# First MLP block by plain products while the weights come; loads, roundings and the first attention in an order written out by hand

## The chip, the cores and the metric

The kernel runs on one core of a Trainium2 chip. Time is device microseconds of one execution. Three timed runs of the kernel before stand beside one execution recorded by the hardware profiler, whose timeline is called the trace. The core's engines work from queues of their own and wait for each other by semaphores: TensorE (PE, with its weight loads PEld), VectorE (DVE), ScalarE (ACT), GpSimd (POOL) and SyncE (SP), which here only issues DMAs.

## The reference

A linear attention without softmax is followed by a two-layer MLP with a leaky ReLU. Batch 8, 8 heads, 576 tokens, head size 64; the MLP sees 4608 tokens of 512 features, 2048 hidden.

```python
kv  = np.einsum('bhsd,bhse->bhde', k, v)
out = np.einsum('bhsd,bhde->bhse', q, kv)
rms = np.sqrt(np.mean(out * out, axis=-1, keepdims=True) + 1e-06)
x   = (out / rms * g_norm).astype(np.float32)       # then (B,H,S,D) -> (B*S, H*D)
h = x @ w_in
g = np.maximum(0.01 * h, h)
return (g @ w_out).astype(np.float32)
```

q, k, v and the result are float32. The weights w_in and w_out come as float64, 8 MB each, and have to be turned into float32 on the chip.

## The kernel before

**Tokens and blocks.** The 4608 tokens are worked off in nine blocks of 512 (`NT`), the eight batches of attention have 576 tokens each, so batch b ends in block b+1. x of a block is kept transposed, `xT` (features on partitions, four sub-tiles `e`, 512 tokens as columns).

**Attention (`attention(b)`, a generator).** Heads go in four pairs p. `load_pair(b, p)` (L87) issues, on SP, two DMAs for k, two for v, and four for q; q is fetched twice, once shifted by 32 columns, so that the DVE's transpose of 32x32 blocks (L198) yields `qT`. Per pair ten small matmuls add up `kv_ps`; a copy (L213) puts it into a block-diagonal `kv`. For each of two pieces of the batch (its columns in block b and in block b+1) four groups of matmuls give `o_ps`; ACT squares it (`sq`, L227) and scales it into `xT` (L228), DVE adds the squares up (L232), a matmul with a matrix of ones (`ss_ps`) sums them per head, ACT takes the root (`rms`, L238), DVE the reciprocal (L239) and the product (L240).

**Weights (`weights()`, a generator).** There are 32 jobs. A job is 512 KB of float64 (`raw`, pool `stage`, two buffers, loaded by SP, L133) that becomes a quarter of one of the 128x1024 tiles `w1`/`w2`. `round_f64` (L120) does this with integer arithmetic: two ACT operations (`add`, `cut`, L137 and L139) and four DVE operations (L140 to L145). Chunk c of the hidden features needs eight jobs in this order: `w1` of half 0 (two jobs), `w1` of half 1 (two), `w2` of half 0 (two), `w2` of half 1 (two).

**MLP.** Each block is computed by a form of Strassen's scheme: `product_h(c)` makes seven products of four 128x256 matmuls from sums of the four quarters of w_in (`sides_w1` on POOL) and of x (`sides_x` on DVE, L245), `product_o(c)` likewise seven from sums of g and w_out. A block has four chunks c, so 56 products. PSUM banks `ha hb hc oa ob oc` hold the products, two more are the attention's.

**What sets the order.** Generators are advanced by `go(steps, n)`. The main loop interleaves `product_h(c)` of a block with `product_o` of the chunk before, one or two steps of the next batch's attention, and, in block 0, the weights. Only the matmuls are held in program order (`keep_in_program_order`); everything else is put in order by the framework's scheduler, which goes by its own estimates. Each engine then executes its list strictly in that order, and a DMA on SP waits there until its target buffer is free. At the start, four rounds of one weight job and two attention steps are written, then the rest of the attention, then the loop.

Of the kernel before, what the change touches and what calls it, by code (L numbers as in the profile page):

```python
# [7 lines left out]
F32 = mybir.dt.float32  # L8
# [12 lines left out]
def kernel(  # L21
# [49 lines left out]
    stage = ctx.enter_context(tc.tile_pool(name="stage", bufs=2))  # L71
# [8 lines left out]

    def matmul(*args, **kw):
        tc.keep_in_program_order(nc.tensor.matmul(*args, **kw))  # L82


    k_ins, v_ins, q_ins = {}, {}, {}

    def load_pair(b, p):  # L87

        for name, src, to in (("k", k, k_ins), ("v", v, v_ins)):
            t = ins.tile([P, 2, JJ, D], F32, tag=f"{name}_in", name=f"{name}_in")
            hs = slice(2 * p, 2 * p + 2)
            nc.sync.dma_start(
                t[:64], src[b, hs, :SLO, :].rearrange("h (p j) d -> p h j d", j=JJ))
            nc.sync.dma_start(
                t[64:, :, :J], src[b, hs, SLO:, :].rearrange("h (p j) d -> p h j d", j=J))
            to[b, p] = t
        t = ins.tile([P, T * D], F32, tag="q_in", name="q_in")
        for l in range(2):  # L100
            for c in range(2):
                r0, n = 64 * l + 32 * c, T * D - 32 * c
                src = q[b, 2 * p + l].rearrange("(t s) d -> t (s d)", s=T)
                nc.sync.dma_start(t[r0:r0 + 32, :n], src[:, 32 * c:])
        q_ins[b, p] = t
# [15 lines left out]
    def round_f64(dst, src):  # L121

        a, n = dst.shape[1:]
        raw = stage.tile([P, a, n, 2], U32, tag="raw", name="raw")
        nc.sync.dma_start(raw.rearrange("p a n two -> p a (n two)"), src.bitcast(U32))  # L133
        raw = raw.rearrange("p a n two -> p (a n) two")
        lo, hi = raw[:, :, 0], raw[:, :, 1]
        add = work.tile([P, a * n], U32, tag="t2k", name="add", bufs=5)
        nc.scalar.activation(add, lo, func=AF.Copy, scale=2.0 ** -29)  # L137
        cut = work.tile([P, a * n], F32, tag="t2k", name="cut", bufs=5)
        nc.scalar.activation(cut, hi.bitcast(F32), func=AF.Copy, scale=2.0 ** -112)  # L139
        nc.vector.tensor_scalar(cut, cut, HIGH_MOST, -HIGH_MOST, op0=ALU.min, op1=ALU.max)  # L140
        tmp = work.tile([P, a * n], U32, tag="t2k", name="tmp", bufs=5)
        nc.vector.tensor_scalar(tmp, cut.bitcast(U32), 3, None, op0=ALU.logical_shift_left)  # L142
        nc.vector.scalar_tensor_tensor(tmp, in0=cut.bitcast(U32), scalar=0x80000000, in1=tmp,  # L143
                                       op0=ALU.bitwise_and, op1=ALU.bitwise_or)
        nc.vector.tensor_tensor(dst.bitcast(U32), tmp.rearrange("p (a n) -> p a n", a=a),  # L145
                                add.rearrange("p (a n) -> p a n", a=a), op=ALU.add)

    w_in_e = w_in.rearrange("(p e) f -> p e f", e=NE)
    w_out_u = w_out.rearrange("(h c u p) m -> h c p u m", h=2, c=NC, p=P)

    def weights():

        for c in range(NC):
            jobs = []
            for h in range(2):
                f0 = h * (DF // 2) + c * U * P
                jobs += [(w1_sb[h][c][:, 2 * a:2 * a + 2, :],
                          w_in_e[:, 2 * a:2 * a + 2, f0:f0 + U * P]) for a in range(2)]
            for h in range(2):
                jobs += [(w2_sb[h][c][:, u:u + 1, :], w_out_u[h, c, :, u:u + 1, :])  # L160
                         for u in range(U)]
            for dst, src in jobs:
                if w_in.dtype == I64:
                    round_f64(dst, src)
                else:
                    nc.sync.dma_start(dst, src)
                yield

    eps_sb = consts.tile([P, 1], F32, name="eps_sb")
    nc.vector.memset(eps_sb, EPS)  # L170

# [19 lines left out]

    def attention(b):

        qT = work.tile([P, NP, S], F32, tag="qT", name="qT")
        kv_ps = ps_att.tile([P, NP, D], F32, tag="att", name="kv_ps")
        for p in range(NP):
            k_in, v_in, q_in = (x.pop((b, p)) for x in (k_ins, v_ins, q_ins))
# [3 lines left out]
            for j in range(JJ):  # L201
                n = P if j < J else 64
                for l in range(2):
                    matmul(kv_ps[64 * l:64 * l + 64, p, :], lhsT=k_in[:n, l, j, :],
                           rhs=v_in[:n, l, j, :], start=(j == 0), stop=(j == JJ - 1))
# [4 lines left out]
        kv = kvs[b % 2]  # L210
        for l in range(2):
            r = slice(64 * l, 64 * l + 64)
            nc.vector.tensor_copy(kv[r, :, :, l, :],  # L213
                                  kv_ps[r].rearrange("p a (i e) -> p a e i", e=NE))
        yield
        for i in (b, b + 1):
            lo, hi = max(i * NT, b * S), min((i + 1) * NT, (b + 1) * S)
            n = hi - lo
            x = block(i)[:, :, lo - i * NT:hi - i * NT]
            sums = None  # L220
            for e in range(NE):
                o_ps = ps_att.tile([P, n], F32, tag="att", name="o_ps")
                for p in range(NP):
# [233 lines left out]
```

## Time and profile before

| | |
|---|---|
| median of three runs (lowest, highest) | 1093.86 us (1093.34, 1098.46) |
| the profiled execution, its own time | 1093.87 us |
| its span, first to last instruction | 1092.2 us |
| mean granted TensorE clock | 0.964 |
| busy: PE, PEld, DVE, ACT, POOL | 992.1, 808.7, 454.0, 270.9, 568.9 us |
| read from HBM, written | 54.27 MB, 9.44 MB |

A line of the timeline reads: start in us from the span's first instruction, duration, engine, line of the code, operation, what is written <- what is read, shape, how many; in brackets the idle time of the engine just before and what ended it. Four fp32 matmuls of 128x256 show as x8, since each is two instructions. A line of the groups ends with busy time in us, mean duration of one in ns, and the idle time of the engine before, with its releasers. A queue (SPq) line is the issuing of DMAs, not their transfer. The rows of stages give length, busy time of PE, PEld, DVE, ACT and POOL with the number of instructions, the granted clock (1.00 is full), the share of DMA busy time and GB/s.

### The profile page before, as it was taken

Reading aid. Unit: us, or ns where it says so; the run is one execution under the profiler, and the core shown is the slowest. Engines: PE = TensorE matmul, PEld = TensorE weight load, DVE = VectorE, ACT = ScalarE, POOL = GpSimd, SP = SyncE. Lnnn points to the kernel's source line nnn. Section 1 sums busy time; section 2 is a strip of 40 time slices with the busy share of each in tenths; the row PEclk is TensorE's granted clock in tenths of the full one; section 3 lists DMA queues with packets and bytes.
Section 4 is the critical chain, followed back from the end, with each engine's and each line's share of the span. In section 5 each row is a group of like instructions: output and inputs, shape, how many; then the busy total and the mean of one; then the engine's idle time right before and its main releaser. Section 6 shows DMA issues by size and latency. Waiting matters only on the chain.

```text
span 1092.2 us, 13409 instructions
## 1 busy us (share of the span) xinstructions
PE 992.1 (91%) x5216; PEld 808.7 (74%) x5216; DVE 454.0 (42%) x617; ACT 270.9 (25%) x498; POOL 568.9 (52%) x441
## 2 busy tenths in 40 slices
PE   2465657999999999999999999999999999999997
PEld 1053445787778877888788878877888788888886
DVE  2485798622462236323632363235322542232223
ACT  0433462113221322122212221222122312111210
POOL 0223334655565556555655565556555655666651
PEclk9686888999999999999999999999999999999999
DMA  8557441240023102310231023101100000001001
GB/s 217 156 142 205 134 153 40 65 118 30 1 65 106 42 1 65 96 52 1 65 96 51 1 65 97 51 1 43 54 30 1 1 10 29 1 1 40 1 1 39
DMA packets 41343, 64.58 MB, mean 59 GB/s; under 512 B 5440, under 2 KB 31040, under 8 KB 41280
## 3 DMA queue, kind: packets, MB, share of 16 engines
q1 hardware_dynamic: 31232, 54.28, 18.2%
q10 hardware_dynamic: 10048, 9.44, 2.6%
q8 instruction: 42, 0.69, 0.3%
q14 instruction: 21, 0.17, 0.1%
HBM read 54.27 MB, written 9.44 MB: 58 GB/s over the span
## 4 chain that ended last, share of the span: by engine, by line
PE 80%; DVE 10%; DMA 4%; issue 2%; ACT 1%; SPq 1%; ACTq 0%; POOL 0%; DVEq 0%
PE h_a L82 22%; PE o_a L82 21%; PE h_c L82 11%; PE o_c L82 10%; PE h_b L82 6%; PE o_b L82 6%; PE o_ps L82 3%; DMA k_in<-in_k_dram 2%; PE kv_ps L82 2%; DVE rms L239 2%; DMA raw<-in_moe_w_in_dram 2%; DVE tmp L143 2%; DVE tmp L142 1%; DVE qT L198 1%; DVE o L245 1%
## 5 line engine op out<-in xcount | busy, mean ns | idle before, releaser
L245 POOL TENSOR_TENSOR wt<-w,wt 128x512 f32<-128x512 f32 x72 | 91.7, 1274 | 151.8 <-PE o_a L82 141.5
L82 PE MATMUL o_a<-wt,gs 128*128 128x256 f32 x576 | 142.5, 391 | 6.7 <-DVE o L245 6.7
L82 PE MATMUL h_a<-xt,ws 128*128 128x256 f32 x576 | 141.9, 390 | 0.0
L245 DVE TENSOR_TENSOR o<-o_a,o 128x512 f32<-128x512 f32 x117 | 80.4, 687 | 143.4 <-PE o_a L82 143.2
L82 PEld LDWEIGHTS o_a<-wt,gs 128*128 128x128 f32 x576 | 106.5, 192 | 37.7 <-issue 19.0
L82 PEld LDWEIGHTS h_a<-xt,ws 128*128 128x128 f32 x576 | 106.9, 192 | 28.0 <-POOL ws L245 7.3
L245 POOL TENSOR_TENSOR gs<-g,g 128x512 f32<-128x512 f32 x72 | 96.6, 1342 | 51.2 <-ACT g L321 47.9
L321 ACT ACTIVATE g<-g 128x512 f32<-128x512 f32 x108 | 68.0, 629 | 147.7 <-DVE g L245 147.5
L245 POOL TENSOR_TENSOR wt<-w,w 128x512 f32<-128x512 f32 x36 | 46.2, 1283 | 98.1 <-PE o_a L82 98.1
L245 POOL TENSOR_TENSOR ws<-ws,w 128x512 f32<-128x512 f32 x36 | 49.6, 1379 | 85.5 <-PE h_a L82 85.2
L245 DVE TENSOR_TENSOR o<-o_c,o 128x512 f32<-128x512 f32 x63 | 43.5, 691 | 95.4 <-PE o_c L82 89.1
L82 PE MATMUL h_a<-xt,w 128*128 128x256 f32 x288 | 70.8, 390 | 9.2 <-DVE g L245 9.2
L82 PE MATMUL h_a<-xT,w 128*128 128x256 f32 x288 | 71.6, 393 | 7.0 <-DVE w L145 7.0
L245 POOL TENSOR_TENSOR ws<-w,w 128x512 f32<-128x512 f32 x36 | 48.3, 1341 | 56.3 <-DVE w L145 55.6
L326 ACT COPY g<-h_a 128x512 f32<-128x512 f32 x36 | 21.1, 585 | 221.7 <-PE h_a L82 209.7
L82 PE MATMUL h_c<-xt,ws 128*128 128x256 f32 x288 | 69.9, 387 | 6.2 <-POOL ws L245 6.2
L245 DVE TENSOR_TENSOR g<-h_b,g 128x512 f32<-128x512 f32 x36 | 24.9, 692 | 115.4 <-PE h_b L82 115.3
L82 PE MATMUL o_a<-wt,g 128*128 128x256 f32 x288 | 68.3, 380 | 2.9 <-DVE o L245 2.9
L82 PE MATMUL o_ps<-qT,kv 128*32 128x64 f32 (+7 forms) x512 | 49.9, 458 | 22.4 <-ACT xT L228 20.8
L82 PEld LDWEIGHTS h_a<-xt,w 128*128 128x128 f32 x288 | 54.8, 194 | 20.3 <-DVE g L245 13.0
L82 PE MATMUL o_c<-wt,gs 128*128 128x256 f32 x288 | 69.1, 383 | 0.0
L82 PE MATMUL o_a<-w,g 128*128 128x256 f32 x288 | 68.1, 379 | 0.8 <-DVE o L245 0.8
(58 smaller groups left out, 1615.2 us busy)
## 6 DMA issues: line engine op xcount, KB each, us to landing
q_in<-in_q_dram SPq DMA_DIRECT2D x64, 144.0 KB, 3.1
out_dram<-o ACTq DMA_DIRECT2D x36, 256.0 KB, 2.2
q_in<-in_q_dram SPq DMA_DIRECT2D x64, 140.0 KB, 3.2
raw<-in_moe_w_in_dram SPq DMA_DIRECT2D x16, 512.0 KB, 4.1
raw<-in_moe_w_out_dram SPq DMA_DIRECT2D x16, 512.0 KB, 3.5
k_in<-in_k_dram SPq DMA_DIRECT2D x32, 160.0 KB, 3.1
v_in<-in_v_dram SPq DMA_DIRECT2D x32, 160.0 KB, 3.2
k_in<-in_k_dram SPq DMA_DIRECT2D x32, 128.0 KB, 3.0
```

The lines of the kernel that those rows point to most:

```text
L82: tc.keep_in_program_order(nc.tensor.matmul(*args, **kw))
L142: nc.vector.tensor_scalar(tmp, cut.bitcast(U32), 3, None, op0=ALU.logical_shift_left)
L143: nc.vector.scalar_tensor_tensor(tmp, in0=cut.bitcast(U32), scalar=0x80000000, in1=tmp, op0=ALU.bitwise_and, op1=ALU.bitwise_or)
L198: nc.vector.transpose(qT[:, p, :].rearrange("p (t s) -> p s t", s=T), q_in.rearrange("p (s d) -> p s d", d=D)[:, :, :32])
L239: nc.vector.reciprocal(rms, rms)
L245: eng.tensor_tensor(out_, a, b_, op=ALU.subtract if minus else ALU.add)
L321: nc.scalar.activation(t, t if src is None else src, func=AF.Prelu, alpha=SLOPE)
L326: nc.scalar.copy(g11, bank)
```

## The change

Block 0's MLP is no longer done by Strassen's scheme. `first_block` computes it in sixteen chunks of 128 hidden features: four 128x512 matmuls into one PSUM bank (`h_ps`, two banks in turn), a leaky ReLU on ACT straight out of PSUM (`gT`), and four 128x512 matmuls that add into four accumulators (`o_acc`). The output matmuls of a chunk stand one chunk later than its h. Between two chunks stand two weight jobs, and from chunk 5 on the steps of batch 1's attention.

```python
def first_block(between):
    accs = [ps_m.tile([P, DM], F32, tag=t, name="o_acc") for t in ("ha", "hb", "oa", "ob")]
    x, last = xTs.pop(0), None
    for n in range(2 * NC * U + 1):
        now = last
        if n < 2 * NC * U:
            c, h, u = n // (2 * U), n // U % 2, n % U
            h_ps = ps_m.tile([P, NT], F32, tag=("hc", "oc")[n % 2], name="h_ps")
            for e in range(NE):
                matmul(h_ps, lhsT=w1_sb[h][c][:, e, u * P:(u + 1) * P], rhs=x[:, e, :],
                       start=(e == 0), stop=(e == NE - 1))
            gT = gpool.tile([P, NT], F32, tag=("g11", "g12", "g21", "g22")[n % 4], name="gT")
            nc.scalar.activation(gT, h_ps, func=AF.Prelu, alpha=SLOPE)
            last = (gT, w2_sb[h][c][:, u, :], n)
        if now is None:
            continue
        for t in range(4):
            matmul(accs[t], lhsT=now[0][:, t * P:(t + 1) * P], rhs=now[1],
                   start=(now[2] == 0), stop=(n == 2 * NC * U))
        between(n)
...
first_attention()
w_steps = weights(4, 2)
load_w(5)
a_steps = tail_of(0, NT, S)

def between(n):
    nonlocal a_steps
    go(w_steps, 2)
    if n == 5:
        go(a_steps)
        load_pair(1, 0)
        load_pair(1, 1)
        a_steps = attention(1)
    if n > 5:
        go(a_steps, 2 if n > 12 else 1)

go(w_steps, 2)
first_block(between)
```

The accumulators are copied out by DVE and ACT in turn. The main loop then runs over blocks 1 to 8, without weight steps; `attention` is as before, apart from being cut into functions (`attention_kv`, `copy_kv`, `outputs`, `divide`, `tail_of`).

Batch 0's attention is written out. Its q is loaded like k and v (once, 288 KB a pair, pairs 0 and 1 by ACT's queue), turned by matmuls with an identity into PSUM, and copied to `qT` by ACT. Its 512 tokens of block 0 go in two halves of 256 columns, with PSUM banks of the MLP; the other 64 columns (`tail_of(0, NT, S)`) come in the first block.

```python
def first_attention():
    for j in range(2):
        load_w(j)
    ...
    for p in range(NP):
        attention_kv(0, p, kv_ps)
        q_in = q_ins.pop((0, p))
        ...
                matmul(to, lhsT=q_in[:n, l, j, :], rhs=ident[:n, :n], start=True, stop=True)
        copy_kv(0, slice(p, p + 1), kv_ps)
        ...
            nc.scalar.copy(to[:, :J, :], q_ps[:, :, r:r + 64])
        if p < 2:
            load_pair(0, p + 2)
            round_w(p)
    load_w(2)
    load_w(3)
    load_w(4)
    nc.scalar.copy(qT[:, :, :SLO].rearrange("p a (t j) -> p a t j", j=JJ)[:, :, :, J], rest)
    ...
    for h in range(2):
        for e in range(NE):
            sums[h] = outputs(0, h * N2, h * N2 + N2, e, sums[h], ps("o_ps"))
            if h == 1 and e == 0:
                divide(0, N2, sums[0], ps("ss_ps"))
    divide(N2, NT, sums[1], ps("ss_ps"))
    round_w(2)
    round_w(3)
```

Loading and rounding of a weight are apart (`load_w`, `round_w`), loads run two to three jobs ahead, and the operations of both, like the loads of q, k and v, are held in program order by `pin`. Roundings now write into the target (`dst`) instead of a `tmp`.

```diff
-    stage = ctx.enter_context(tc.tile_pool(name="stage", bufs=2))
+    stage = ctx.enter_context(tc.tile_pool(name="stage", bufs=3))
...
+    pin = tc.keep_in_program_order
...
-        add = work.tile([P, a * n], U32, tag="t2k", name="add", bufs=5)
-        nc.scalar.activation(add, lo, func=AF.Copy, scale=2.0 ** -29)
+        add = work.tile([P, a * n], U32, tag="t2k", name="add", bufs=4)
+        pin(nc.scalar.activation(add, lo, func=AF.Copy, scale=2.0 ** -29))
...
+    def weights(j, ahead):
+        for n in range(j, len(w_jobs)):
+            if n + ahead < len(w_jobs):
+                load_w(n + ahead)
+            round_w(n)
+            yield
...
+    warm = consts.tile([P, 1], F32, name="warm")
+    nc.scalar.activation(warm, eps_sb, func=AF.Sqrt)
...
-        t1, t2, t3, t4 = (work.tile([P, 2, N2], F32, tag=f"xt{i}", name=f"xt{i}")
-                          for i in range(1, 5))
+        t1, t2, t4 = (work.tile([P, 2, N2], F32, tag=f"xt{i}", name=f"xt{i}")
+                      for i in (1, 2, 4))
+        t3 = b12
```

How the lists of the engines look now is shown at three places. First ACT at the start, before: the third and fourth roundings (`add`, `cut` from `raw`) stand around the first square of the attention's outputs.

```order
L137 ACTIVATE add<-raw 128x512
L139 ACTIVATE cut<-raw 128x512
L137 ACTIVATE add<-raw 128x512
L139 ACTIVATE cut<-raw 128x512
L137 ACTIVATE add<-raw 128x512
L139 ACTIVATE cut<-raw 128x512
L227 ACTIVATE sq<-o_ps 128x512
L228 ACTIVATE xT<-o_ps,g_sb 128x512
L137 ACTIVATE add<-raw 128x512
L139 ACTIVATE cut<-raw 128x512
L227 ACTIVATE sq<-o_ps 128x512
```

ACT at the same place in the changed program, from the second rounding on: the copies of the turned q, then the outputs.

```order
L148 ACTIVATE add<-raw 128x512
L150 ACTIVATE cut<-raw 128x512
L310 COPY qT<-q_ps 128x4x64 x4
L317 COPY qT<-rest_ps 128x4x64
L245 ACTIVATE sq<-o_ps 128x256
L246 ACTIVATE xT<-o_ps,g_sb 128x256
L245 ACTIVATE sq<-o_ps 128x256
L246 ACTIVATE xT<-o_ps,g_sb 128x256
```

The third and fourth roundings have moved behind the last `rms` of the attention.

Second, PE from the end of the first attention into the MLP, before: `o_ps` and `ss_ps` belong to batch 0's attention, `h_a`, `h_c`, `h_b` to block 0's products, `kv_ps` to batch 1.

```order
L82 MATMUL ss_ps<-sq,same 128x512
L82 MATMUL o_ps<-qT,kv_138 32x64 x16
L82 MATMUL ss_ps<-sq,same 128x64
L82 MATMUL h_a<-xT,w_0_0_116 128x256 x4
L82 MATMUL h_c<-xt_362,ws_370 128x256 x4
L82 MATMUL h_b<-xT,w_0_0_116 128x256 x4
L82 MATMUL kv_ps<-v_in,k_in 64x64 x10
L82 MATMUL h_a<-xt_363,ws_371 128x256 x4
```

PE at this place now; `w_h_c` in the names is the tile of half h and chunk c, w1 for `h_ps` and w2 for `o_acc`.

```order
L84 MATMUL o_ps<-qT,kv_139 32x256 x20
L84 MATMUL ss_ps<-sq,same 128x256
L84 MATMUL o_ps<-qT,kv_139 32x256 x12
L84 MATMUL ss_ps<-sq,same 128x256
L84 MATMUL h_ps<-xT,w_0_0_112 128x512 x8
L84 MATMUL o_acc<-w_0_0_120,gT 128x512 x4
L84 MATMUL h_ps<-xT,w_1_0_116 128x512 x4
L84 MATMUL o_acc<-w_0_0_120,gT 128x512 x4
```

The last 64 columns and the first kv of batch 1 have moved behind chunk 5, and products of 256 columns have become matmuls of 512.

Third, ACT in the middle of block 0. Before, four or five roundings in a row stood between the products' copies (`g11` and so on, here `g_650`, `g_653`):

```order
L137 ACTIVATE add<-raw 128x512
L139 ACTIVATE cut<-raw 128x512
L326 COPY g_650<-h_a 128x512
L328 COPY g_653<-h_c 128x512
L137 ACTIVATE add<-raw 128x512
L139 ACTIVATE cut<-raw 128x512
L321 ACTIVATE g_650<-g_650 128x512
```

ACT of the changed program at chunks 6 to 9, whose relus are the `gT` rows (chunk 6, then 7 and 8 together, then 9):

```order
L488 ACTIVATE gT<-h_ps 128x512
L148 ACTIVATE add<-raw 128x512
L150 ACTIVATE cut<-raw 128x512
L148 ACTIVATE add<-raw 128x512
L150 ACTIVATE cut<-raw 128x512
L488 ACTIVATE gT<-h_ps 128x512 x2
L148 ACTIVATE add<-raw 128x512
L150 ACTIVATE cut<-raw 128x512
L148 ACTIVATE add<-raw 128x512
L150 ACTIVATE cut<-raw 128x512
L488 ACTIVATE gT<-h_ps 128x512
```

From the pair of relus on, the two roundings written between chunks n and n+1 stand behind the relu of chunk n+1; those behind the last row shown hold `w2` of chunk 8.

More of the change, by code (lines that the diff above doesn't have):

```diff
@@ L135, in round_f64 @@
         lo, hi = raw[:, :, 0], raw[:, :, 1]
-        add = work.tile([P, a * n], U32, tag="t2k", name="add", bufs=5)
[L137 to L141, printed above, removed]
```

221 lines of the change are left out of this document (130 added, 91 removed).

## The prediction

> **What bounds the kernel now.** I read the slices of the span first, then busy time by stage, then the timeline of the first 217 us.
>
> ```profile
> PE   2465657999999999999999999999999999999997
> PEclk9686888999999999999999999999999999999999
> 0.00:59.90 59.90, 18.84 (x148) 8.13 (x149) 25.63 (x34) 14.13 (x27) 7.98 (x13) 0.79 0.66 170
> 59.90:216.00 156.10, 111.11 (x534) 85.49 (x534) 116.55 (x167) 60.38 (x107) 62.17 (x46) 0.83 0.46 129
> 216.00:326.70 110.70, 109.08 (x597) 88.82 (x597) 42.38 (x56) 26.20 (x50) 63.35 (x48) 1.00 0.19 53
> 326.70:1092.20 765.50, 753.04 (x3941) 626.24 (x3939) 269.45 (x362) 170.20 (x314) 435.41 (x334) 1.00 0.13 37
> ```
>
> The page's two rows of 40 slices show TensorE half idle, at a reduced clock, in the first eight slices, and full afterwards. The stage rows (length, then busy PE, PEld, DVE, ACT, POOL; clock; DMA share; GB/s) put numbers to it: from 216 us on PE is busy 862 of 876 us, so only less PE work could shorten that part. Before 216 us PE is busy 130 of 216 us, part of it at the lower clock: here order and waiting decide. The boundary is block 1's first product:
>
> ```profile
> 216.03 1.89 PE L82 MATMUL h_a<-xT,w 128*128 128x256 f32 x8
> 217.76 1.89 PE L82 MATMUL o_a<-wt,g 128*128 128x256 f32 x8
> 223.03 0.95 PE L82 MATMUL kv_ps<-v_in,k_in 128*64 128x64 f32 x20
> 246.23 1.89 PE L82 MATMUL o_a<-wt,g 128*128 128x256 f32 x8
> ```
>
> One product of four 128x256 matmuls follows the next after 217.76 - 216.03 = 1.73 us. At 216.03 eight output products of block 0 are still due (217.76 is its c=2's last, 246.23 its c=3's last): 8 x 1.73 = 13.8 us.
>
> I therefore split the changed span into **A**, up to block 1's first product (before: 216.0), and **B**, the rest (before: 1092.2 - 216.0 = 876.2).
>
> **Part A, until x of block 0 is ready.**
>
> ```profile
> 24.28 1.53 PE L82 MATMUL kv_ps<-v_in,k_in 128*64 128x64 f32 x20 [3.30 <-DMA v_in<-in_v_dram]
> 26.82 1.26 DVE L198 STREAM_TRANSPOSE qT<-q_in 128x576 f32<-128x576 f32 x1
> 40.19 0.66 ACT L137 ACTIVATE add<-raw 128x512 uint32<-128x512 uint32 x1 [10.69 <-DMA raw<-in_moe_w_in_dram]
> 41.43 0.43 DVE L140 TENSOR_SCALAR cut<-cut 128x512 f32<-128x512 f32 x1 [9.56 <-ACT cut L139]
> 42.52 1.93 PE L82 MATMUL o_ps<-qT,kv 128*32 128x512 f32 x8 [10.77 <-ACT xT L228]
> 56.17 2.29 DVE L240 TENSOR_TENSOR xT<-xT,rms 128x2048 f32<-128x2048 f32 x1
> 59.94 3.25 PE L82 MATMUL h_a<-xT,w 128*128 128x256 f32 x8
> ```
>
> The fourth pair of heads arrives by about 26.8, yet the attention outputs stand until 42.5: ACT holds a rounding whose raw load was issued behind two pairs of batch 1. x is complete at 58.5. The new order takes batch 1's pairs out of this stretch and puts the third rounding behind the attention, so that wait goes.
>
> Next late is the fourth pair itself. It moves 4 x 864 KB and two raws of 512 KB, against 4 x 1144 KB and one raw ahead of it before (q came twice, in rows of 144 and 140 KB; now once, 288 KB).
>
> ```profile
> 15.00:20.00 5.00, 0.55 (x10) 0.58 (x12) 3.11 (x5) 1.21 (x2) 0.00 (x0) 1.00 1.09 252
> q_in<-in_q_dram SPq DMA_DIRECT2D x64, 144.0 KB, 3.1
> L198 DVE STREAM_TRANSPOSE qT<-q_in 128x576 f32<-128x576 f32 x32 | 39.5, 1245 | 15.2 <-DMA q_in<-in_q_dram 14.9 <-PE o_ps L82 0.2
> ```
>
> That is 608 KB less, 2.5 us at the 252 GB/s of a saturated window: q of pair 3 lands near 24.5. Turning q on TensorE isn't in the trace. Its ten matmuls have twice kv's columns, and kv's ten took 1.53 us cold: between 1.5 and 3.1, I take 2.5. The ACT copies out of PSUM (two, and one for the rest) resemble the 128x256 squares below: 1.2 us together. The Sqrt table, the identity and the quarters of kv's copy lie beside the loads and cost nothing. So outputs begin at 24.5 + 2.5 + 1.2 + 0.5 (first products) = 28.7.
>
> The Trainium skill, "VectorE: DVE Perf Modes" (Rules for kernel authors), calls the DVE transpose the fastest for 32x32 within a bank, which speaks against this edit. By it alone the fourth pair would be done 3.7 - 1.25 = 2.4 us sooner; but the DVE form needs the doubled q, 4 x 280 KB or 4.6 us more of the saturated DMA, so by the rows here the edit gains about 2 us.
>
> Then, in halves of 256 columns:
>
> ```profile
> L227 ACT ACTIVATE sq<-o_ps 128x256 f32<-128x256 f32 x8 | 3.1, 384 | 17.4 <-PE o_ps L82 17.4
> L228 ACT ACTIVATE xT<-o_ps,g_sb 128x256 f32<-128x256 f32 x8 | 3.7, 468 | 0.0
> L232 DVE TENSOR_TENSOR sq<-sq 128x256 f32<-128x256 f32 x6 | 3.5, 580 | 1.2 <-ACT sq L227 1.2
> L82 PE MATMUL ss_ps<-sq,same 128*128 128x256 f32 x4 | 1.2, 379 | 0.0
> L238 ACT ACTIVATE rms<-ss_ps,eps_sb 128x256 f32<-128x256 f32 x2 | 0.9, 474 | 4.8 <-PE ss_ps L82 4.8
> L239 DVE RECIPROCAL rms<-rms 128x256 f32<-128x256 f32 x2 | 3.4, 1724 | 0.2 <-ACT rms L238 0.2
> L240 DVE TENSOR_TENSOR xT<-xT,rms 128x1024 f32<-128x1024 f32 x2 | 3.1, 1572 | 0.0
> ```
>
> Half 0: four squares with scalings (0.8 each, 3.2), sum 0.6, ss 0.7, rms 0.5: reciprocal from 33.7. DVE then sets the pace: 1.7 + 0.6 + 1.6 + 2 x 0.6 = 5.1, to 38.8; half 1's ss and rms 1.1, reciprocal 1.7, product 1.6: **x at 43** (38 if the loads lead, 47 if the pairs come at the old 26.8 and everything stays cold).
>
> **Part A, the first block.** Sixteen chunks of eight 128x512 matmuls are, by columns, four of the products above each: 4 x 1.73 = 6.9 us; 16 of them 110.6 (Strassen's 56 products took 96.9, so 13.7 are added). Batch 1's attention between them: four kv at 0.95 (223.03), four 448-wide outputs at 0.96 (145.70, below), and the rest, 64 and 128 wide with three ss, 2.8 by their columns and some 3.4 because they are short: 11.
>
> The weights must keep up, two jobs a chunk or 3.5 us a job.
>
> ```profile
> 118.06 8.71 SPq L133 DMA_DIRECT2D raw<-in_moe_w_in_dram  x4
> 118.71 0.42 DVE L140 TENSOR_SCALAR cut<-cut 128x512 f32<-128x512 f32 x1
> 119.16 0.43 DVE L142 TENSOR_SCALAR tmp<-cut 128x512 uint32<-128x512 uint32 x1
> 119.63 0.69 DVE L143 SCALAR_TENSOR_TENSOR tmp<-cut,tmp 128x512 uint32<-128x512 uint32 x1
> 120.35 0.69 DVE L145 CUSTOM_DVE_ANT_0 w<-tmp,add 128x1024 uint16<-128x1024 uint16 x1
> 120.96 0.42 DVE L140 TENSOR_SCALAR cut<-cut 128x512 f32<-128x512 f32 x1
> L142 DVE TENSOR_SCALAR tmp<-cut 128x512 uint32<-128x512 uint32 x32 | 21.2, 663 | 1.0
> L321 ACT ACTIVATE g<-h_a 128x512 f32<-128x512 f32 x36 | 21.5, 597 | 59.1 <-PE h_a L82 48.1 <-POOL gs L245 11.0
> ```
>
> Before, SP issued four raws in 8.7 us (2.2 a job) with two buffers; after has three. A rounding takes DVE 120.96 - 118.71 = 2.25. So neither is the bound as long as nothing stands between. What can stand between is the fixed order on ACT, where each rounding sits behind a chunk's relu (gT). Through chunk 7 a relu and then two roundings follow each other, and the weights are a chunk ahead. From chunk 8 the order has two relus together, and each pair of roundings stands one relu later. Hence these waits on PE:
>
> - chunk 5: block 1's first 64 columns run in one piece; PE waits for squares and sums behind two roundings: **3** (0 to 6).
> - out of chunk 8 (and again of chunk 12): its w2 is rounded behind the relu of the chunk just computed, which is itself at PE's tail: relu 0.6, ACT to DVE 41.43 - 40.19 = 1.2, DVE 2.25, or **4.1**; for chunk 12 one of the two ACT steps is done earlier, **3.5**. (Each 0 if the relu were not ahead.)
> - chunk 12's h needs two roundings behind relu 11, with 3.5 us of PE work as cover: 0.6 + 1.2 + 2 x 2.25 - 3.5 = 2.8; **2.8**.
> - the end: the last sums wait behind two evictions and a transpose (0.7 + 0.7 + 1.25): **3**.
>
> ```profile
> 140.32 1.99 PE L82 MATMUL o_a<-wt,g 128*128 128x256 f32 x8 [1.13 <-DVE o L245]
> 145.70 0.96 PE L82 MATMUL o_ps<-qT,kv 128*32 128x448 f32 x8
> 172.99 3.78 PE L82 MATMUL h_a<-xt,w 128*128 128x256 f32 x8 [5.83 <-DVE g L245]
> 176.56 2.91 PE L82 MATMUL o_c<-wt,gs 128*128 128x256 f32 x8
> ```
>
> After 5.83 us of idleness two products took 3.78 and 2.91 for 1.99 and 1.89: 2.8 us lost to the lower clock; after 1.13 nothing. I add 2.6 at the start and, between the ends 0 and 2.8, 1.2 for each of the two long waits. Waits and clock: 3 + 4.1 + 3.5 + 2.8 + 3 + 2.4 = 18.8, beside the 2.6.
>
> A = 43 + 2.6 + 110.6 + 11 + 18.8 = **186** (before 216).
>
> **Part B.** 876.2 - 13.8 = 862.4. Block 1's first stage now runs without output products between. One product waits for the eviction of the bank before it, and pairs 2 and 3 of batch 2 are wanted 5 us sooner after their loads go out: +4 (0 to 8). TensorE's order in the later blocks is unchanged; xt3 written into x's own columns removes no DVE work; four instead of five t2k buffers and loads in written order (k, v before q, each waiting on SP for its buffer) lie beside a PE that is 98% busy there: 0 (between -1 and +5, if a late k or v stopped PE once a block). POOL loses block 0's sides, off the path.
>
> Sum: 186 + 862.4 + 4 = 1052.4 of span; the profiled execution took 1093.87 beside its span of 1092.2, so 1.7 more: **1054 us**, 3.6% faster. That execution stands at the median of the runs shown (1093.86), so nothing is shifted.
>
> **Rivals.**
>
> 1. *Unbroken chunks.* ACT and DVE catch up early enough that only some 4 us of waits remain: 1054 - 15 = 1039. For: the roundings alone leave DVE a third idle. Against: the fixed order of ACT shows the two relus.
> 2. *DVE becomes the bound.* L142 took 0.66 in the mean of its 32, against 0.43 undisturbed: some were slowed by half as much again or more. If a rounding takes 3.3, its 26 jobs need 86 us, and batch 1's attention adds four transposes (5.0) and, by columns, 576/256 of a half's sums, reciprocal and product, 2.25 x (3 x 0.58 + 1.72 + 1.57) = 11.3: together 102, where 13 chunks with their share of attention need 13 x 7.6 = 99. That is 3 more, and the four waits behind roundings each grow by about that backlog: +16, 1070. Against: the 2.25 above, and that block 0 loses its side sums on DVE and its accumulations.
> 3. *Slower: loads one at a time.* A load waits on SP for the reading of the buffer three jobs earlier, and batch 1's pairs stand ahead of it in the queue.
>
> ```profile
> raw<-in_moe_w_in_dram SPq DMA_DIRECT2D x4, 512.0 KB, 5.6
> ```
>
> If each of 26 jobs costs its whole landing of 5.6 us (median in the first 60 us) instead of 3.5, the block grows by 26 x 2.1 = 55: 1109. It decides for slower from 3.5 + 46/26 = 5.3 us a job. Against: the 2.2 above.
> 4. *It does nothing.* What is saved at the start returns as waits for weights and A stays 216 long: about 1093.
>
> **How the numbers follow.** Forecast 0.60 (1054), unbroken 0.18, DVE-bound 0.14, slower 0.05, nothing 0.03. Half a per cent, 5.5 us, is about what a measurement of this kernel can tell from no change. Faster: 0.60 + 0.18 + 0.14 = 0.92; same 0.03; slower 0.05. The range goes from x at 38 with few waits (1054 - 5 - 16 = 1033) to x at 47 with DVE-bound waits (1054 + 4 + 16 = 1074).
>
> **What would show it.** h_ps starting near 43 with ACT free of raw waits before it; h_ps and o_acc groups of four at 3.45 us; PE's idle times named ACT gT or DVE w at chunks 8 and 12; block 1's h_a near 186; from there to the end 866. The prediction is wrong if raws land late behind batch 1's pairs (ACT add waiting for DMA), if DVE has no gaps in the first block, or if B isn't 862 to 870.

## The result and the profile after

| | before | after |
|---|---|---|
| median (lowest, highest) | 1094.03 us (1093.34, 1098.46) | 1046.33 us (1043.93, 1048.25) |
| span of the profiled execution | 1092.2 us | 1046.5 us |
| mean granted clock | 0.964 | 0.987 |
| busy: PE, DVE, ACT, POOL | 992.1, 454.0, 270.9, 568.9 us | 997.6, 420.4, 266.2, 503.7 us |

The changed kernel takes 0.9555 of the time before, with a 95% interval of [0.9523, 0.9587]: 48 us less. The profiled execution, 1048.25 us, is the slowest of the four. One execution of strassen_free below (1113.27 us, clock 0.918) and one of the kernel before beside later runs (1772.43 us, clock 0.595) ran in a slower state and are left out of the numbers below.

The page's rows of 40 slices for the changed kernel (each digit a busy share, then the granted clock, in tenths):

```profile
PE   4699889899999999999999999999999999999997
PEclk8899999999999999999999999999999999999999
```

Only the first two slices are still thin, where seven were. The stages of the changed kernel, with the same columns as before (length; busy PE, PEld, DVE, ACT, POOL; clock; DMA share; GB/s), cut where x of block 0 is ready (40.0), at block 1's first product (184.5), and at 330:

```profile
0.00:40.00 40.00, 18.06 (x228) 13.34 (x229) 14.52 (x28) 16.37 (x37) 2.36 (x11) 0.88 0.62 164
40.00:184.50 144.50, 131.58 (x439) 56.22 (x439) 92.05 (x147) 52.72 (x101) 11.23 (x8) 0.94 0.51 150
184.50:330.00 145.50, 142.80 (x819) 116.89 (x818) 52.55 (x69) 37.09 (x69) 83.85 (x65) 1.00 0.28 74
330.00:1046.50 716.50, 705.20 (x3656) 586.20 (x3655) 261.26 (x344) 160.02 (x296) 406.29 (x312) 1.00 0.12 34
```

Before, x was ready at 59.9 and block 1 began at 216.0 with 13.8 us of block 0's output products still due. So the 45.7 us that the span lost are 59.94 - 40.03 = 19.9 at the start, (156.1 + 13.8) - 144.5 = 25.4 in the first block, and the small rest behind. From 184.5 on, TensorE idles 2.7 + 11.3 = 14.0 us; before it idled 1.6 + 12.5 = 14.1 there. Nothing is gained or lost in that part.

TensorE's timeline at the places that the prediction spoke of:

```profile
23.84 1.09 PE L84 MATMUL q_ps<-ident,q_in 128*64 128x128 f32 x16
24.87 0.33 PE L84 MATMUL rest_ps<-ident,q_in 64*64 64x64 f32 x4
26.64 2.37 PE L84 MATMUL o_ps<-qT,kv 128*32 128x256 f32 x40 [1.44 <-ACT qT L317]
...
40.03 9.11 PE L84 MATMUL h_ps<-xT,w 128*128 128x512 f32 x16 [3.70 <-DVE xT L259]
50.57 3.67 PE L84 MATMUL o_acc<-w,gT 128*128 128x512 f32 x8 [1.43 <-DVE w L157]
54.08 3.60 PE L84 MATMUL h_ps<-xT,w 128*128 128x512 f32 x8
57.51 3.60 PE L84 MATMUL o_acc<-w,gT 128*128 128x512 f32 x8
...
84.43 0.41 PE L84 MATMUL ss_ps<-sq,same 128*128 128x64 f32 x2 [1.14 <-DVE sq L249]
84.68 5.35 PE L84 MATMUL h_ps<-xT,w 128*128 128x512 f32 x8
...
118.10 5.37 PE L84 MATMUL o_acc<-w,gT 128*128 128x512 f32 x8 [4.25 <-DVE w L157]
141.27 1.98 PE L84 MATMUL h_ps<-xT,w 128*128 128x512 f32 x4 [0.20 <-DVE w L157]
154.91 6.26 PE L84 MATMUL o_acc<-w,gT 128*128 128x512 f32 x8 [3.70 <-DVE w L157]
184.20 0.46 PE L84 MATMUL ss_ps<-sq,same 128*128 128x128 f32 x2 [1.59 <-DVE sq L249]
184.50 1.89 PE L84 MATMUL h_a<-xT,w 128*128 128x256 f32 x8
```

The reader is to see two things. Four 128x512 matmuls follow the next four after 57.51 - 54.08 = 3.43 us, so a chunk is 6.86 us as long as nothing stands between. And the two long waits, 4.25 us at chunk 8 and 3.70 us at chunk 12, each have a slow group behind them (5.37 and 6.26 for 3.60 us, at a granted clock of 0.67 and 0.58), so they cost more than their length.

What made the wait at chunk 8 is seen in ACT's and DVE's rows just ahead of it:

```profile
113.89 0.60 ACT L488 ACTIVATE gT<-h_ps 128x512 f32<-128x512 f32 x1 [5.08 <-PE h_ps L84]
114.38 0.65 ACT L148 ACTIVATE add<-raw 128x512 uint32<-128x512 uint32 x1
114.92 0.66 ACT L150 ACTIVATE cut<-raw 128x512 f32<-128x512 f32 x1
115.61 0.43 DVE L151 TENSOR_SCALAR cut<-cut 128x512 f32<-128x512 f32 x1 [2.18 <-ACT cut L150]
```

ACT had been idle for 5.08 us when it took the relu of the chunk that TensorE had just ended. Only behind it came the rounding of the weights that TensorE needed at once. Its raw data was there (no wait for DMA); the order alone held it back.

### The profile page after: what moved, and what is told of

Its sections match the earlier page's. It is cut to its first block, busy times and chain, and to the rows that moved or that the text cites. A ratio compares the mean times of both kernels' runs of the same rounds, so it can differ in the third digit from the quotient of the medians.

```text
span 1046.5 us, 13143 instructions
## 1 busy us (share of the span) xinstructions
PE 997.6 (95%) x5138; PEld 772.7 (74%) x5138; DVE 420.4 (40%) x586; ACT 266.2 (25%) x502; POOL 503.7 (48%) x395
## 4 chain that ended last, share of the span: by engine, by line
PE 90%; DVE 5%; DMA 1%; ACT 1%; issue 1%; SPq 1%; ACTq 0%; DVEq 0%
PE o_a L84 21%; PE h_a L84 21%; PE h_c L84 10%; PE o_c L84 10%; PE o_acc L84 5%; PE o_b L84 5%; PE h_b L84 5%; PE h_ps L84 5%; PE o_ps L84 3%; PE kv_ps L84 2%; DVE rms L258 2%; PE ss_ps L84 1%; DVE w L155 1%; DVE w L154 1%; DVE w L157 1%
## 5 line engine op out<-in xcount | busy, mean ns | idle before, releaser
L84 PE MATMUL o_a<-wt,gs 128*128 128x256 f32 x512 | 124.8, 386 | 2.9 <-DVE o L335 2.9
L84 PEld LDWEIGHTS o_a<-wt,gs 128*128 128x128 f32 x512 | 94.1, 190 | 28.5 <-issue 12.9
L335 POOL TENSOR_TENSOR ws<-w 128x512 f32<-128x512 f32 x32 | 44.2, 1382 | 143.3 <-PE h_c L84 141.5
L335 POOL TENSOR_TENSOR gs<-g,g 128x512 f32<-128x512 f32 x64 | 84.9, 1327 | 18.6 <-ACT g L412 15.8
L412 ACT ACTIVATE g<-g 128x512 f32<-128x512 f32 x96 | 60.4, 629 | 129.4 <-DVE g L335 128.8
L84 PE MATMUL o_acc<-w,gT 128*128 128x512 f32 x128 | 62.2, 631 | 9.4 <-DVE w L157 9.4
L84 PE MATMUL h_ps<-xT,w 128*128 128x512 f32 x128 | 62.3, 632 | 3.9 <-DVE xT L259 3.7
L84 PE MATMUL h_a<-xT,ws 128*128 128x256 f32 x256 | 62.4, 387 | 0.0
L84 PE MATMUL h_a<-xt,ws 128*128 128x256 f32 x256 | 62.4, 386 | 0.0
L335 POOL TENSOR_TENSOR ws<-w,w 128x512 f32<-128x512 f32 x32 | 42.4, 1325 | 39.9 <-DVE w L157 39.2
L84 PE MATMUL h_a<-xT,w 128*128 128x256 f32 x256 | 60.6, 379 | 0.0
L84 PE MATMUL h_c<-xT,ws 128*128 128x256 f32 x256 | 60.5, 379 | 0.0
```

The lines of the kernel that those rows point to most:

```text
L84: pin(nc.tensor.matmul(*args, **kw))
L335: eng.tensor_tensor(out_, a, b_, op=ALU.subtract if minus else ALU.add)
L412: nc.scalar.activation(t, t if src is None else src, func=AF.Prelu, alpha=SLOPE)
```

## The experiments

The ratios below are each to the kernel before, measured beside it. To compare kernels inside the profile I also use **stage S**: from the sums of block 0's second half (the second 256-column `ss_ps`, the same instruction in every kernel with the new start) to block 1's first product. In the changed kernel it goes from 35.66 to 184.50, 148.8 us. Where output products of block 0 are still due behind it, 13.8 us are added.

### 1. pin_relu: the relu in the fixed order

```diff
-                nc.scalar.activation(gT, h_ps, func=AF.Prelu, alpha=SLOPE)
+                pin(nc.scalar.activation(gT, h_ps, func=AF.Prelu, alpha=SLOPE))
```

> Chunk n's relu on ACT is put into the fixed order, behind the roundings that stand ahead of it in the program. Theory A (the wait out of chunks 8 and 12 comes from a relu that stood ahead of the roundings): PE's waits of 4.25 and 3.70 us there fall below 1 us, the groups behind them take 3.6 instead of 5.37 and 6.26, and the time is about 12 us less than that of the changed kernel: 1034 (1031 to 1038). Theory B (the raw loads are late there, behind batch 1's pairs in SP's queue): ACT waits for DMA ahead of the pinned relu, PE waits 3 us or more at the same places, and the time is 1043 to 1052.

Measured: 1035.59 us median, ratio 0.9474 [0.9457, 0.9492], against 0.9555 for the changed kernel: 0.0081 x 1093 = 9 us less. TensorE's timeline of this kernel where the two waits were, at the output matmuls of chunks 8 and 12, and the row of its first block:

```profile
113.83 3.60 PE L84 MATMUL o_acc<-w,gT 128*128 128x512 f32 x8
...
144.55 3.60 PE L84 MATMUL o_acc<-w,gT 128*128 128x512 f32 x8
```

```profile
41.86:171.47 129.61, 124.34 (x438) 54.16 (x439) 92.01 (x147) 53.56 (x101) 11.23 (x8) 0.99 0.59 168
```

No row between 88 and 169 us has a wait, and no group is slow. Stage S shrank from 148.8 to 134.0 us. So theory A holds: the free relu that slipped ahead was the whole of both waits. Of the 14.8 us, 12.4 are the two waits and the clock lost behind them (4.25 + 3.70 + 1.77 + 2.66), and 1.7 the clock that was lost at chunk 5 and here was not. The timed gain, 9 us by the ratios and 10.7 by the medians, is smaller: x was ready 1.8 us later in this execution, and the changed kernel's profile is that of its slowest execution. The moment when x is ready lay between 40.0 and 42.4 in four profiles with the same order at the start (40.03, 41.86 here, 40.15 in spread_tail and 42.38 in stage2). ACT did wait for raw loads eight times here, 10.3 us together, but TensorE did not feel it.

### 2. q_on_dve: batch 0's q turned by DVE

```diff
-        if b == 0:
-            q_ins[b, p] = load_rows(nc.scalar if p < 2 else nc.sync, q[b, hs], "q")
-            return
...
-                    matmul(to, lhsT=q_in[:n, l, j, :], rhs=ident[:n, :n], start=True, stop=True)
...
+            nc.vector.transpose(
+                qT[:, p, :].rearrange("p (t s) -> p s t", s=T),
+                q_in.rearrange("p (s d) -> p s d", d=D)[:, :, :32])
```

> Batch 0's q is loaded twice over, in four DMAs a pair (1144 instead of 864 KB a pair), and turned by DVE as before; all else as in the changed kernel. Theory A (the doubled load costs more than the turning): x of block 0 is ready 1 to 4 us later (41 to 44 instead of 40.0) and the time is 2 us more (0 to 5): 1048. Theory B (the rule that the DVE transpose is the fastest way decides): x is ready 2.4 us sooner, 37.6, and the time is 1044.

Measured: 1048.88 us median, ratio 0.9604 [0.9580, 0.9629]. TensorE's timeline of this kernel:

```profile
25.40 1.53 PE L84 MATMUL kv_ps<-v_in,k_in 128*64 128x64 f32 x20 [4.98 <-DMA v_in<-in_v_dram]
...
44.46 9.04 PE L84 MATMUL h_ps<-xT,w 128*128 128x512 f32 x16 [3.70 <-DVE xT L257]
```

The last pair's v arrives at 25.4, while in the changed kernel TensorE began that pair's kv at 22.53 without a wait; the doubled q is loaded beside them. x is ready at 44.5, against 40.0 to 42.4 with the q turned on TensorE. By the medians the kernel is 2.6 us slower than the changed one, by the ratios 5, and the two intervals touch. Theory A holds in its sign, and in its size within the spread of the start. The Trainium skill ("VectorE: DVE Perf Modes", Rules for kernel authors) calls the DVE transpose the fastest for 32x32; that is a rule for the operation alone, which this run does not test: here the layout that this transpose needed cost a second load of q.

### 3 and 4. strassen_first and strassen_free: the new start without plain products

```diff
-    first_block(between)
...
-    for i in range(1, NB):
+    for i in range(NB):
...
+                go(w_steps, 1)
```

> The new start and the new loads and roundings stay, but block 0's MLP goes by the seven products of the other blocks (56 products of 1.73 us and side sums instead of 16 chunks of 6.9 us), with batch 1's attention between them. Theory A (plain products give the 25 us of the stage, as they need no side sums of the weights): x ready at 40, the stage from there as long as before, time 1066 to 1076. Theory B (the order and the third raw buffer give them): the side sums no longer wait, the stage is up to 14 us shorter than with plain products, time 1032 to 1044.

In the second one the six operations of a rounding are no longer held in the fixed order:

```diff
-        pin(nc.scalar.activation(add, lo, func=AF.Copy, scale=2.0 ** -29))
+        nc.scalar.activation(add, lo, func=AF.Copy, scale=2.0 ** -29)
...
```

> As strassen_first, but the roundings on ACT and DVE are no longer held in the written order; loads are. Theory A (the 22.7, 11.1 and 7.1 us that TensorE waited for attention there came from the fixed order of ACT and DVE, and the 9.4 us for side sums did not): those waits shrink, the wait for POOL's sums stays, and the time is 1055 to 1070, still 10 us or more above the plain products. Theory B (without the fixed order Strassen's 13.7 us fewer of products win): 1032 to 1044. Theory C (the order is as bad either way): 1080 to 1088.

Measured: 1084.61 us, ratio 0.9922 [0.9904, 0.9941], and 1078.42 us (three runs), ratio 0.9859 [0.9838, 0.9881]. TensorE's five longest waits behind x in strassen_first, from its timeline, then the square on ACT that ended the longest of them, then a sum of weights on POOL in strassen_free:

```profile
50.45 3.78 PE L84 MATMUL h_c<-xt,ws 128*128 128x256 f32 x8 [9.35 <-POOL ws L335]
87.87 0.44 PE L84 MATMUL o_ps<-qT,kv 128*32 128x64 f32 x8 [22.68 <-ACT xT L246]
123.06 1.53 PE L84 MATMUL kv_ps<-v_in,k_in 128*64 128x64 f32 x20 [5.63 <-DMA v_in<-in_v_dram]
161.84 3.21 PE L84 MATMUL o_ps<-qT,kv 128*32 128x448 f32 x16 [11.11 <-ACT xT L246]
176.68 1.83 PE L84 MATMUL ss_ps<-sq,same 128*128 128x448 f32 x2 [7.10 <-DVE sq L249]
```

```profile
87.39 0.22 ACT L245 ACTIVATE sq<-o_ps 128x64 f32<-128x64 f32 x1 [2.75 <-DVE w L155]
```

```profile
43.97 8.47 POOL L335 TENSOR_TENSOR ws<-w,w 128x512 f32<-128x512 f32 x1 [40.97 <-DVE w L157]
```

Stage S is 37.02 to 207.60 plus 13.8, or 184.4 us, and 177.4 us in strassen_free: 36 and 29 us longer than with plain products, and the first time lies 9 us above theory A's range (1066 to 1076). The earlier x is given back nearly whole. Of TensorE's waits in this stretch of strassen_first, 60.3 us together, 9.4 are for POOL's sums of weights, 5.6 for a load of v, and 43.2 for batch 0's and batch 1's attention. ACT had six roundings between the outputs that TensorE ended at 65.2 and their squares at 87.39, and it waited for DVE between them. Raw data was there: ACT waited 2.5 us for it in the whole kernel. Without the fixed order of the roundings the wait of 22.7 us became 8.0, but the one for POOL's sums grew to 13.4 (a sum that takes 1.3 us elsewhere took 8.47), and the others stayed or grew, so theory C came nearest. Freeing the roundings thus does not make up the difference, and theory B of the first and of the second run is out; other orders of attention and roundings were not tried.

### 5 and 6. plain_no_w and strassen_no_w: the same two, with the weights there

Neither kernel loads or rounds the weights.

```diff
+    for dst, src in w_jobs:
+        nc.vector.memset(dst, 0.02)
     def load_w(j):
-        dst, src = w_jobs[j]
...
     def round_w(j):
...
```

> The changed kernel without loading and rounding the weights: all weight tiles are set to 0.02 by DVE at the start, and nothing of the 32 jobs is left on SP, ACT and DVE. It measures the first block with its weights there. The 16 chunks of 6.9 us and 11 us of attention stand, the waits for weights (1.4, 4.25, 3.70 us and the clock behind them) go: 124 to 130 us from x to block 1 instead of 144.5, and x is ready some 4 us sooner, as two raw loads less stand ahead of pair 3. Time 1020 to 1030.

> strassen_first without loading and rounding the weights (all weight tiles 0.02, as in plain_no_w). Theory A (Strassen's block loses only because its side sums and its attention stand behind weights that are still coming): with the weights there its 13.7 us fewer of products show, the stage takes at most as long as the plain one, and the time is 1005 to 1025, below plain_no_w. Theory B (the block is slow by its own sums and by attention's chain, weights or not): waits of 10 us or more stay in it, and the time is above plain_no_w by 10 us or more.

Measured: 1038.13 us, ratio 0.9499 [0.9478, 0.9520], and 1023.57 us, ratio 0.9366 [0.9351, 0.9380]. The rows of the first block of plain_no_w, strassen_no_w and, with its weights coming, strassen_first, in this order:

```profile
45.78:175.76 129.98, 125.88 (x439) 54.82 (x439) 20.18 (x27) 19.18 (x44) 0.00 (x0) 0.97 0.15 43
```

```profile
39.90:148.40 108.50, 100.79 (x567) 80.88 (x567) 48.50 (x60) 28.30 (x60) 54.30 (x42) 0.95 0.17 44
```

```profile
37.90:207.60 169.70, 109.35 (x568) 84.93 (x567) 128.97 (x180) 65.81 (x120) 70.22 (x50) 0.80 0.46 126
```

Stage S, with the 13.8 us of products still due in the Strassen kernels:

| | weights coming | weights there |
|---|---|---|
| plain products | 148.8 (134.0 with the relu in order) | 134.4 |
| Strassen's products | 184.4 (177.4 without the fixed order) | 122.8 |

With the weights there Strassen is 11.6 us shorter, near the 13.7 us that its fewer products are worth. With the weights coming it is 36 us longer. Theory A is right as it was put: what plain products save is not work of TensorE but waits, for sums of weights and for attention, behind the weights. Four of Strassen's seven products need sums of several pieces of the weights, which must all be rounded first; a plain product needs the pieces of its own chunk alone. Yet that is the smaller part of the waits seen. The larger is attention behind roundings on ACT and DVE, and DVE is busy for 129 of the 170 us there (92 of 144.5 in the changed kernel). The two runs leave out both the loads and the work of rounding, so they do not tell which of these is how much of the 36 us. Plain products with the relu in order take as long as with all weights there; as plain_no_w lost 1.75 us of the clock at chunk 5 and pin_relu did not, pin_relu's block has some 2 us left to gain from its weights, about its wait of 1.95 us for the first `w2` piece. The absolute time of plain_no_w missed its range (1020 to 1030), because x was ready at 45.8: the 32 fills of weight tiles keep DVE until 18.2 us, ahead of the copies of kv.

### 7. old_start: the old attention, then plain products

```diff
-    first_attention()
-    w_steps = weights(4, 2)
+    first, w_steps, a_steps = weights(0, 0), weights(4, 2), attention(0)
+    for _ in range(4):
+        go(first, 1)
+        go(a_steps, 2)
+    go(a_steps)
...
```

> Batch 0's attention by the old code (q twice, DVE transpose, 512 columns at once, batch 1's first pairs loaded in it, each rounding's load directly ahead of it), then the plain products of the changed kernel. Theory A (the two parts of the change add up): x of block 0 is ready at 59 to 60 instead of 40.0, the block behind it takes as long as in the changed kernel, time 1066 (1063 to 1069). Theory B (half of the earlier x is given back as waits for weights, which a later start does not have): the chunks run without the waits of 1.4, 1.7, 4.2 and 3.7 us and their slower groups, time 1050 to 1058.

Measured: 1054.40 us, ratio 0.9646 [0.9629, 0.9663]: some 8 to 10 us more than the changed kernel, not 20. From TensorE's timeline, then ACT's relus of chunks 9 and 10, then the row of the first block:

```profile
165.28 3.67 PE L84 MATMUL o_acc<-w,gT 128*128 128x512 f32 x8 [3.70 <-DVE w L154]
```

```profile
130.45 0.60 ACT L485 ACTIVATE gT<-h_ps 128x512 f32<-128x512 f32 x1 [5.09 <-PE h_ps L84]
138.39 0.60 ACT L485 ACTIVATE gT<-h_ps 128x512 f32<-128x512 f32 x1 [7.34 <-PE h_ps L84]
```

```profile
62.39:192.27 129.88, 124.40 (x405) 53.76 (x406) 80.41 (x135) 49.80 (x92) 5.19 (x4) 0.98 0.49 144
```

x is ready at 62.4, 22 us later, and the block takes 129.9 us instead of 144.5. The time is theory B's: of 22 us, 15 come back. Its reason fits only in part. About 3 us are the last 64 columns, done before x here, and 1.75 the clock lost behind them; 1.4 are the wait at the first chunk; 6.0 the wait at chunk 8 with its slow group; and 2.7 the clock behind the wait at chunk 12, which itself stayed (3.70 us). The wait at chunk 8 went because the scheduler put another relu ahead: the two without roundings between them are here those of chunks 9 and 10, not 7 and 8. So it is the order again, not shown to be the later start. In the changed kernel a part of the earlier start was spent on waits that experiment 1 shows to be avoidable. Beside the kernel before, plain products without the new start give 3.5% (0.9646), the new start without plain products 0.8% (0.9922), both 4.45% (0.9555).

### 8. stage2: two raw buffers

```diff
-    stage = ctx.enter_context(tc.tile_pool(name="stage", bufs=3))
+    stage = ctx.enter_context(tc.tile_pool(name="stage", bufs=2))
```

> The changed kernel with two raw buffers instead of three. Theory A (the third buffer lets the raw loads run ahead): each load is issued one rounding later, ACT waits for DMA ahead of roundings, TensorE's waits for weights grow at several chunks: 5 to 25 us more, 1051 to 1070. Theory B (a load of 2.2 us a job is fast enough against 3.5 us of a job's share of the products): within 3 us of the changed kernel.

Measured: 1048.33 us, ratio 0.9593 [0.9576, 0.9611]; the interval overlaps that of the changed kernel. In the profile x is ready at 42.4, and stage S is 37.97 to 185.63, 147.7 us, against 148.8. Theory B holds: the third buffer is worth nothing that shows in the block. With the relus in order, where ACT did wait for raw loads, two buffers were not tried.

### 9 to 12. On top of pin_relu: what is left

early_half computes chunks 0 and 1 for columns 0 to 255 first; spread_tail puts batch 0's last 64 columns into chunks 2 to 5, a step in each; combo has both and rounds the first `w2` piece ahead of the second half's `w1`; combo2 puts the next two roundings behind chunk 0's relu.

```diff
+                    for s in range(2):
+                        for m in range(2):
+                            for e in range(NE):
+                                matmul(h_01[m][:, s * N2:s * N2 + N2], ...
...
+        if 1 < n <= 5:
+            go(a_steps, 2 if n == 5 else 1)
...
+    w_jobs[2:5] = w_jobs[4:5] + w_jobs[2:4]
...
+                between(0)
...
-    go(w_steps, 2)
```

> pin_relu, with the products of chunks 0 and 1 split by columns: columns 0 to 255 of x, which are ready about 5 us before the rest, go first. Theory A (TensorE's 3.70 us wait for the second half and its low clock behind it are lost time): 3.5 us of products move into the wait, and the 16 matmuls that took 8.6 lose less of the clock: 3.5 to 5 us less than pin_relu, 1031. Theory B (the weights of the next step are the bound there): the wait of 1.95 us behind those products grows to 5 or 6, and the time stays within 1 us of pin_relu's.

> pin_relu, with batch 0's last 64 columns spread over chunks 2 to 5, a step in each, instead of in one piece behind chunk 5. Theory A: the short waits there (0.44 and 1.14 us) go, nothing else moves: 1.6 us less than pin_relu, 1034. Theory B (the squares then stand between roundings that are needed sooner): waits of 1 us or more come up at the first chunks, and the time is the same or up to 3 us more.

> early_half and spread_tail together, and the first w2 piece is loaded and rounded ahead of the two w1 pieces of the second half, as the product that waited 1.95 us needs it first. If the gains add up: 3.5 to 5, 1.6 and 2 us less than pin_relu, 1027 (1025 to 1031). If raw loads become the bound (ACT waiting for DMA ahead of roundings, with the block started sooner): waits for weights come up at chunks 2 to 10, and the time is 1031 to 1036.

> combo, with the roundings of jobs 4 and 5 put behind chunk 0's relu in the fixed order: TensorE waited 2.03 us for that relu, which stood behind four roundings on ACT. Theory A: that wait goes and nothing comes in its place: 2 us less than combo, 1028. Theory B (the w1 pieces of chunk 2 are then late by as much): the same time as combo within 1 us.

| kernel | median, us | ratio and interval | stage S, us |
|---|---|---|---|
| pin_relu | 1035.59 | 0.9474 [0.9457, 0.9492] | 134.0 |
| early_half | 1036.30 | 0.9480 [0.9461, 0.9499] | 138.7 |
| spread_tail | 1033.91 | 0.9464 [0.9448, 0.9480] | 134.0 |
| combo | 1029.87 | 0.9421 [0.9406, 0.9435] | 129.4 |
| combo2 | 1029.49 | 0.9420 [0.9402, 0.9437] | 129.8 |

early_half's timeline of TensorE, then combo's:

```profile
36.75 8.76 PE L84 MATMUL h_ps<-xT,w 128*128 128x256 f32 x32
51.17 6.72 PE L84 MATMUL o_acc<-w,gT 128*128 128x512 f32 x8 [5.66 <-DVE w L157]
```

```profile
38.54 3.62 PE L84 MATMUL h_ps<-xT,w 128*128 128x256 f32 x16
42.32 3.72 PE L84 MATMUL h_ps<-xT,w 128*128 128x256 f32 x16 [0.16 <-DVE xT L260]
48.07 3.70 PE L84 MATMUL o_acc<-w,gT 128*128 128x512 f32 x8 [2.03 <-ACT gT L500]
```

Alone, the early half is theory B: the matmuls moved into the wait for x, and the wait behind them grew from 1.95 to 5.66 us, because the first `w2` piece is the third to be rounded; the group behind it then ran slowly. With that piece rounded first, and the columns spread, stage S of combo is 4.6 us shorter than pin_relu's, and its time lies in the range for gains that add up (1025 to 1031). spread_tail alone gains nothing in the stage (the wait for the sums stayed, 1.2 us), so its 1.7 us of median show no more than that x came 1.7 us sooner in its profile; the two intervals overlap. combo2's wait of 2.03 us for the relu went, and one of 1.41 us for the next weights took its place: theory B again. combo beats both kernels of this study: 0.9421 against 0.9555.

## Why the prediction was right, point by point

| term | predicted, us | measured, us |
|---|---|---|
| x of block 0 ready | 43 | 40.0 |
| lower clock at the start | 2.6 | 9.11 - (3.43 + 3.60) = 2.1 |
| 16 chunks | 110.6 | 16 x 6.86 = 109.8 |
| batch 1's attention and small gaps | 11 | 13.5 (the rest of 184.5) |
| out of chunk 0 | 0 | 1.4 |
| chunk 5 | 3 | 1.7 |
| out of chunks 8 and 12 | 4.1 and 3.5 | 4.25 and 3.70 |
| h of chunk 12 | 2.8 | 0.2 |
| the end | 3 | 1.6 |
| lower clock behind waits | 2.4 | 1.75 + 1.77 + 2.66 = 6.2 |
| **A** | **186** | **184.5** |
| **B** | **866.4** | **862.0** |

- **The start.** The mechanism was right: without batch 1's pairs and the third rounding in the way, the outputs ran from 26.64 on, where before two of the four groups had stood until 42.5. The size was 3 us off. The fourth q was there by 23.84 (24.5 was predicted), but turning it took 1.09 + 0.33 us of TensorE, not 2.5, and DVE's chain from the first reciprocal (31.49) to the end took 8.4 us, not 9.3.
- **The waits behind the relus.** They stood at the places and had the lengths that were read out of ACT's order, and experiment 1 shows that order to be their cause.
- **Mis-sized terms.** The clock lost three times, not twice, and more each time. Chunk 12's h needed the second rounding two matmuls (1.7 us) later than was assumed, and a group of attention outputs (0.9 us) gave more cover, which hid it. The waits at chunk 5 and at the end were each some 1.4 us shorter. That these errors, of up to 3.8 us each, nearly cancel in A is luck, and the clock behind the wait at chunk 12 (2.66 us) is chance: the same wait cost nothing in old_start and q_on_dve.
- **A wait that was missed.** The product of chunk 0 waited 1.4 us for its first `w2` piece, which is rounded last of the three that are due. It cost little there, but it is what swallowed early_half.
- **Part B.** The step that failed is the allowance of 4 us for block 1's start. A wait of 1.5 us for v did come up, but the idle time of the whole part stayed at 14.0 us against 14.1. With A 1.5 us shorter too, the span was 5.9 us below the sum; the median lies another 1.9 us below the profiled execution, so 1054 was 7.7 us too high.
- **The rivals.** The first, unbroken chunks, is not what the changed kernel did, but what pin_relu came to (1035.6 against 1039). The second, DVE as the bound, is out: DVE was busy for 92 of 144.5 us. The third is out: ACT waited for a raw load once in the whole changed kernel, for 1.0 us, and with one raw buffer less the block did not get longer. The fourth was out by the 45.7 us.

What the prediction did not ask is whether Strassen's products would have gained from the new start as well. Hardly, in the order tried here: 1084.6 us, 0.8% less than before.

## What to carry to other kernels

A scheme with fewer multiplications can lose while its operands are still being made ready: its sums wait for several pieces, and they and everything else queue behind that work on the same engines. Try the plain scheme there and the clever one behind it, and test it by leaving that work out. Where one engine's operations are partly fixed in order, look at what is not fixed: a single free operation that slips ahead of the work TensorE waits for cost 9 us here. When work is moved into a wait, ask first what the next instruction waits for.

## What the hardware did that was not expected

**The same wait costs the clock or does not.** Behind 3.70 us of idleness a group took 6.26 us in the changed kernel (154.91, granted clock 0.58) and 3.67 in old_start (165.28, clock 1.00). At chunk 5 the changed kernel lost 1.75 us at 84.68 (clock 0.67) behind waits of 0.44, 0.15 and 1.14 us; pin_relu, with nearly the same waits, lost nothing (clock 1.00):

```profile
84.35 0.79 PE L84 MATMUL o_ps<-qT,kv 128*32 128x64 f32 x16 [0.44 <-ACT xT L246]
86.28 0.41 PE L84 MATMUL ss_ps<-sq,same 128*128 128x64 f32 x2 [1.14 <-DVE sq L249]
86.52 3.65 PE L84 MATMUL h_ps<-xT,w 128*128 128x512 f32 x8
```

The Trainium skill ("TensorE: Matmul & The Clock Gate", Part 1) says that the clock is set by how busy TensorE was of late, in a window that runs freely; that one wait can come out both ways agrees with it. It speaks of an idle window, though, and in the 3.0 us ahead of 84.68 TensorE was busy for some 1.3.

**DVE's roundings slow down while POOL works.** In the changed kernel POOL formed block 1's sums of weights as soon as these were rounded, 140 us before they were needed. POOL's and then DVE's rows:

```profile
42.22 1.38 POOL L335 TENSOR_TENSOR ws<-w,w 128x512 f32<-128x512 f32 x1 [39.22 <-DVE w L157]
45.41 1.39 POOL L335 TENSOR_TENSOR ws<-w 128x512 f32<-128x512 f32 x1 [1.82 <-DVE w L157]
46.88 1.33 POOL L335 TENSOR_TENSOR ws<-ws,w 128x512 f32<-128x512 f32 x1
48.28 1.59 POOL L335 TENSOR_TENSOR ws<-w,ws 128x512 f32<-128x512 f32 x1
```

```profile
40.25 0.43 DVE L154 TENSOR_SCALAR w<-cut 128x512 uint32<-128x512 uint32 x1
42.50 1.38 DVE L154 TENSOR_SCALAR w<-cut 128x512 uint32<-128x512 uint32 x1
45.70 1.38 DVE L154 TENSOR_SCALAR w<-cut 128x512 uint32<-128x512 uint32 x1
47.12 1.64 DVE L155 SCALAR_TENSOR_TENSOR w<-cut,w 128x512 uint32<-128x512 uint32 x1
48.78 1.64 DVE L157 CUSTOM_DVE_ANT_0 w<-w,add 128x1024 uint16<-128x1024 uint16 x1
```

Beside POOL's sums the operation of 0.43 us takes 1.38, those of 0.69 take 1.64, and the rounding from 45.25 to 50.4 takes 5.2 us instead of 2.25. Between and behind the sums, with POOL idle, the same operations took 0.69 (43.91) and 0.43 us (50.79). The slowed rounding is the one that TensorE waits for at 50.57. The Trainium skill ("SBUF — State Buffer", Who interferes with whom) has the two engines share a pair of ports that one of them holds at a time; the times agree with that. That this is the cause is read from the times standing side by side; holding POOL's sums back until block 0 is done was not tried.
